# A gated mix of dilated attention and a token MLP on one core: the third w2 load issued ahead of twelve on-chip copies

## The chip, the cores and the metric

The kernel runs on one core of a Trainium2 chip. The metric is device microseconds of one execution. Runs come with the mean clock that TensorE was granted. Before the change: 178.16 us, median of 3 runs (177.43 to 179.45).

## The reference

The reference mixes two branches over x (2048 tokens, 512 features) with a gate per token. Branch A is attention with 32 heads of 16, in which each token looks at 8 earlier tokens at distance 0, 2, ..., 14. Branch B is an MLP along the token axis. Cut to what matters:

```
q, k, v = x @ wqkv                                    # 32 heads of 16
attn = softmax(q . k[s - 2w], w = 0..7)
a = (sum_w attn * v[s - 2w]) @ wo
u = gelu(layernorm(x)^T @ w1 + b1)                    # 512 x 1792, w1: 2048 x 1792
b = (u @ w2 + b2)^T                                   # w2: 1792 x 2048
g = sigmoid(x . gate_w)
out = g * a + (1 - g) * b
```

## The kernel before

The kernel lists its operations with their dependencies and lets a small list scheduler, run when the kernel is built, fix the order on each of the five instruction streams. Of the operations that are ready, the one with the earliest start goes first; among equals, the one with the smaller key, so that a priority of -100 is worth 300 us of critical path:

```python
st = max(clock[e], rtime[op.idx])
k = (st, -bl[op.idx] + 3.0 * op.prio, op.idx)   # bl: longest path to the end
```

All transfers go through one queue, that of SyncE (SP). Two kinds of them matter. The softmax weights are computed in one layout (ATT) and needed in another (ER), chunk by chunk of 512 tokens. So they are copied from SBUF to SBUF, four copies per chunk; the copies of chunks 1 to 3 are twelve, of 288 KB each:

```python
def ld_er(c, r0, nr, rd, nm):
    ds = sch.dsem(nm)
    for g in range(4):
        src = bass.AP(ATT.tensor, ATT.offset + 32 * c * pst5 + r0 * SC, [[pst5, 32], [1, nr * SC]])
        dst = bass.AP(ER.tensor, ER.offset + g * pst5 + (c * (NW + 1) + r0) * SC, [[4 * pst5, 32], [1, nr * SC]])
        sch.dma("sp", mk_dma(dst, src), 32 * nr * SC * 2, ds, reads=rd, writes=["%s_%d" % (nm, g)], deps=er_al, name="d_%s_%d" % (nm, g), prio=-100)
# ... chunk 0 in two halves (er0a, er0b), then its row of reciprocal sums (er0r), then:
for c in range(1, 4):
    ld_er(c, 0, NW + 1, ["att_0", "att_1", "rs_0", "rs_1"], "er%d" % c)
# ... VectorE: per chunk two products of 4.4 us and six smaller steps (the avm to avn steps)
```

The second MLP product takes w2 in eight loads of 896 KB, each for two blocks of 128 tokens, through three buffers. I call the loads w2_0 to w2_7. The third, w2_2, has a buffer of its own that has been free for a long time, so nothing but its place in the queue holds it back:

```python
def ld_w2(j2):
    ds = sch.dsem("w2_%d" % j2)
    al = w2_al[0 if j2 < 2 else 1] if j2 < 3 else ()
    op = sch.dma("sp", mk_dma(W2S[j2 % 3], w2v[:, :, 256 * j2:256 * j2 + 256]), F * 256 * 2, ds,
                 writes=["w2s%d" % (j2 % 3)], deps=al, after=(d_w1[-1:] + d_w2[-1:]) if j2 < 3 else (), name="d_w2_%d" % j2)
    ...
# ... for token block i: two halves (7 matmuls each) with w2, and later 4 matmuls with wo
for half in range(2):
    last_main[0] = A("pe", f_ph3(i, bank, half), 1.515, reads=["ut%d" % ft for ft in ...] + ["w2s%d" % (j2 % 3)], ...)
if i % 2 == 1 and j2 + 3 <= 7:
    ld_w2(j2 + 3)
A("pe", f_wo(i, bank), 0.865, reads=["ot%d" % (i // 4), "wo"], ...)
```

Token block i takes its matmuls with w2 at L840 and those with wo at L849. Blocks 4 and 5 use w2_2. Blocks 12 to 15 need the last chunk of attention from VectorE.

## Time and profile before

| what | value | read from |
|---|---|---|
| span; TensorE busy | 176.4 us; 168.1 us | busy times of the page |
| longest wait of TensorE | 3.79 us, for a DMA of w2 | PE timeline |
| w2_2: issue; landing | 113.16; 121.59 us | SP timeline; landings in the trace |
| er1: landing; needed by VectorE | 105.74; 106.1 us | landings; VectorE's timeline |
| matmuls of 512 columns, 14 in a row | 3.02 us, so 0.216 each | chain of waits |

A landing is the time at which the last DMA engine of a transfer (or group of four copies) counts up its semaphore; the trace holds these times one by one (16 for w2_2, 64 for the four copies of er1).

The first lines to look at are the busy tenths of the page: 40 slices of 4.4 us. PEclk is the granted TensorE clock in tenths.

```profile
PE   7999999999999999999999999974999999999993
DVE  0755369999889996559999999999999999992000
PEclk9999999999999999999999999997899999999999
DMA  5989989930000080809999989989735738001023
```

In the middle of the span TensorE is full except in two slices, the 27th and the 28th, where it falls to 7 and 4. In the 28th and 29th PEclk falls too. The PE timeline of that stretch (start, length, instruction, count, and in brackets the idle time before it and what ended it):

```profile
103.66 2.11 PE L800 MATMUL ps<-arena 128*128 128x512 bf16 x9
105.61 12.25 PE L840 MATMUL ps<-arena 128*128 128x512 bf16 x56
121.64 3.54 PE L840 MATMUL ps<-arena 128*128 128x512 bf16 x8 [3.79 <-DMA arena<-in_B_w_dram]
```

The first 56 matmuls are blocks 0 to 3, four times 14. The next ones wait until w2_2 has landed. Then something else is odd: 8 matmuls fill 3.54 us, which is 0.44 us each and not 0.216. The table of windows (busy time of each engine per stretch, granted clock, DMA share) shows why:

```profile
core 0: us, PE busy (x) PEld busy (x) DVE busy (x) ACT busy (x) POOL busy (x), PEclk, DMA share, GB/s
105.00:117.00 12.00, 12.00 (x57) 5.45 (x56) 11.96 (x4) 0.69 (x1) 0.00 (x0) 1.00 0.97 195
117.00:121.60 4.60, 0.85 (x4) 0.20 (x2) 4.57 (x5) 0.00 (x0) 0.00 (x0) 1.00 0.96 283
121.60:125.00 3.40, 3.36 (x8) 1.19 (x9) 3.33 (x3) 0.00 (x0) 0.00 (x0) 0.50 1.19 290
125.00:130.00 5.00, 5.00 (x25) 2.27 (x24) 5.00 (x2) 0.00 (x0) 0.00 (x0) 1.00 0.29 75
```

Why was w2_2 late? Some lines of the chain of waits and of the SP timeline, in which each SPq line is the issue of a transfer:

```profile
96.71 0.59 SPq L439
...
109.93 1.57 SPq L439
111.51 0.04 issue
111.55 1.57 SPq L439
113.12 0.04 issue
113.16 8.43 DMA arena<-in_B_w_dram
121.59 0.05 issue
121.64 9.36 PE ps L840 x35
```

```profile
91.66 21.46 SPq L439 DMA_DIRECT2D arena<-arena  x16
113.16 7.83 SPq L439 DMA_DIRECT2D arena<-in_B_w_dram  x3
```

The sixteen copies (four of er0r, twelve of er1 to er3) occupy the queue from 91.66 to 113.12. The first issue takes 3.10 us, the next five 0.59 us each, and the later ones mostly about 1.57 us, close to the pace at which the copies land (er1 at 105.74, er2 at 111.29 and er3 at 117.29 us, so 1.4 to 1.5 us a copy). A copy landed 5.8 us after its issue (median of the twelve). Only then does w2_2 go out. VectorE, meanwhile, works through its 32 attention steps without a gap:

```profile
88.14 71.92 DVE L776 TENSOR_TENSOR arena<-arena 128x8192 bf16<-128x8192 bf16 x32
```

### The profile page before, as it was taken

Reading aid. Unit: us, or ns where it says so; the run is one execution under the profiler, and the core shown is the slowest. Engines: PE = TensorE matmul, PEld = TensorE weight load, DVE = VectorE, ACT = ScalarE, POOL = GpSimd, SP = SyncE. Lnnn points to the kernel's source line nnn. Section 1 sums busy time; section 2 is a strip of 40 time slices with the busy share of each in tenths; the row PEclk is TensorE's granted clock in tenths of the full one; section 3 lists DMA queues with packets and bytes.
Section 4 is the critical chain, followed back from the end, with each engine's and each line's share of the span. In section 5 each row is a group of like instructions: output and inputs, shape, how many; then the busy total and the mean of one; then the engine's idle time right before and its main releaser. Section 6 shows DMA issues by size and latency. Waiting matters only on the chain.

```text
span 176.4 us, 2143 instructions
## 1 busy us (share of the span) xinstructions
PE 168.1 (95%) x892; PEld 79.4 (45%) x892; DVE 139.7 (79%) x118; ACT 66.3 (38%) x94; POOL 0.9 (0%) x8
## 2 busy tenths in 40 slices
PE   7999999999999999999999999974999999999993
PEld 2965445455444444444444444421444444444441
DVE  0755369999889996559999999999999999992000
ACT  2376666866285202499231111000002111112174
POOL 1000000000000000000000000000000000000000
PEclk9999999999999999999999999997899999999999
DMA  5989989930000080809999989989735738001023
GB/s 169 324 177 256 156 249 327 291 78 6 0 1 5 8 232 4 238 5 282 231 308 290 197 196 194 190 224 288 183 99 142 204 90 241 30 30 33 30 80 128
DMA packets 43102, 27.42 MB, mean 155 GB/s; under 512 B 7893, under 2 KB 42325, under 8 KB 42709
## 3 DMA queue, kind: packets, MB, share of 16 engines
q1 hardware_dynamic: 43092, 27.28, 62.4%
q8 instruction: 7, 0.11, 0.3%
q14 instruction: 3, 0.02, 0.0%
HBM read 18.88 MB, written 2.10 MB: 119 GB/s over the span
## 4 chain that ended last, share of the span: by engine, by line
PE 58%; SPq 17%; DMA 11%; DVE 8%; ACT 4%; issue 1%
PE ps L840 22%; PE ps L586 14%; SPq L439 12%; PE ps L800 10%; PE ps L849 8%; DMA arena<-in_B_w_dram 5%; SPq L460 4%; PE ps L668 4%; DMA arena<-in_A_x_dram 4%; DMA arena<-in_A_wqkv_dram 3%; DVE arena L713 3%; DVE arena L776 2%; DVE arena L761 2%; ACT arena L727 1%; ACT L727 1%
## 5 line engine op out<-in xcount | busy, mean ns | idle before, releaser
L776 DVE TENSOR_TENSOR arena<-arena 128x2048 bf16<-128x2048 bf16 (+2 forms) x32 | 71.5, 2287 | 0.4
L840 PE MATMUL ps<-arena 128*128 128x512 bf16 x224 | 51.8, 388 | 3.8 <-DMA arena<-in_B_w_dram 3.8
L800 PE MATMUL ps<-arena 128*128 128x512 bf16 x224 | 48.9, 379 | 0.0
L586 PE MATMUL ps<-arena 128*128 128x512 bf16 x176 | 38.9, 379 | 0.6 <-DMA arena<-in_A_x_dram 0.5
L840 PEld LDWEIGHTS ps<-arena 128*128 128x128 bf16 x224 | 22.2, 100 | 31.7 <-DMA arena<-in_B_w_dram 4.3
L661 DVE TENSOR_TENSOR arena<-arena 128x8192 bf16<-128x8192 bf16 x8 | 35.0, 4418 | 1.3 <-ACT arena L597 1.3
L800 PEld LDWEIGHTS ps<-arena 128*128 128x128 bf16 x224 | 21.7, 98 | 26.8 <-issue 0.8
L867 ACT ACTIVATE arena<-ps,arena 128x512 bf16<-128x512 f32 x16 | 12.4, 778 | 55.4 <-PE ps L849 54.9
L586 PEld LDWEIGHTS ps<-arena 128*128 128x128 bf16 x176 | 19.6, 114 | 19.0 <-ACT arena L594 0.9
L597 ACT ACTIVATE arena<-ps 128x512 bf16<-128x512 f32 x32 | 19.0, 597 | 7.1 <-PE ps L586 6.9
L813 ACT ACTIVATE arena<-ps,arena 128x512 bf16<-128x512 f32 x14 | 9.6, 687 | 30.8 <-PE ps L800 30.7
L849 PE MATMUL ps<-arena 128*128 128x512 bf16 x64 | 15.4, 379 | 0.0
L551 DVE BATCH_NORM_STATS2 arena<-arena 128x6 f32<-128x512 bf16 x16 | 9.9, 681 | 6.6 <-DMA arena<-in_A_x_dram 6.6
L849 PEld LDWEIGHTS ps<-arena 128*128 128x128 bf16 x64 | 6.2, 98 | 7.6
L713 DVE TENSOR_TENSOR arena<-arena 128x256 bf16<-128x256 bf16 (+4 forms) x16 | 7.9, 506 | 2.0 <-ACT arena L727 1.7
L594 ACT ACTIVATE arena<-ps 128x512 bf16<-128x512 f32 x12 | 7.2, 596 | 3.5 <-PE ps L586 3.5
L668 PE MATMUL ps<-arena 128*32 128x512 bf16 x128 | 7.5, 380 | 0.0
L698 ACT ACTIVATE arena<-ps 128x1024 bf16<-128x1024 f32 x4 | 4.0, 1021 | 5.0 <-PE ps L638 3.8
L570 DVE TENSOR_SCALAR arena<-arena 128x512 bf16<-128x512 bf16 x16 | 5.3, 406 | 0.0
L668 PEld LDWEIGHTS ps<-arena 128*32 128x32 bf16 x128 | 3.1, 97 | 4.1 <-DVE arena L713 0.4
L513 PE MATMUL ps<-arena 128*128 128x512 bf16 x9 | 4.0, 603 | 1.1 <-POOL arena L426 1.1
L542 DVE COPY arena<-ps 128x512 bf16<-128x512 bf16 x2 | 0.8, 425 | 4.0 <-PE ps L525 3.9
(50 smaller groups left out, 40.2 us busy)
## 6 DMA issues: line engine op xcount, KB each, us to landing
arena<-in_B_w_dram SPq DMA_DIRECT2D x7, 1024.0 KB, 6.8
arena<-in_B_w_dram SPq DMA_DIRECT2D x8, 896.0 KB, 8.9
arena<-arena SPq DMA_DIRECT2D x12, 288.0 KB, 5.8
arena<-in_A_x_dram SPq DMA_DIRECT2D x4, 512.0 KB, 5.1
out_dram<-arena SPq DMA_DIRECT2D x16, 128.0 KB, 1.7
arena<-in_A_wqkv_dram SPq DMA_DIRECT2D x3, 512.0 KB, 4.6
arena<-arena SPq DMA_DIRECT2D x8, 128.0 KB, 3.1
arena<-in_A_wo_dram SPq DMA_DIRECT2D x1, 512.0 KB, 7.7
```

Source lines behind the costliest of these rows:

```text
L439: return lambda e: e.dma_start(dst, src)
L551: A("dve", (lambda t_: (lambda e: e.bn_stats(out=ST6[:, t_, :], in_=X[:, t_, :])))(t), 0.7, reads=["x%d" % t], writes=["st6_%d" % t], name ...
L586: ins = e.matmul(ps[:, bank, :], lhsT=lhsT, rhs=XT[:, sb, dt, :], start=(dt == 0), stop=(dt == 3))
L597: return lambda e: e.activation(out=dst, in_=ps[:, bank, :], func=AF.Copy)
L661: return lambda e: e.tensor_tensor(out=PBL[buf], in0=in0, in1=in1, op=ALU.mult)
L668: ins = e.matmul(ps[32 * c:32 * c + 32, 4 + wl, :], lhsT=RP, rhs=PBL[buf][:, wl, c * 512:(c + 1) * 512], start=(dl == 0), stop=(dl == 3), ...
L713: return A("dve", lambda e: e.tensor_tensor(out=o_, in0=a_, in1=b_, op=op_), dur, reads=rd, writes=wr, name=nm)
L776: A("dve", lambda e: e.tensor_tensor(out=o_, in0=a_, in1=b_, op=op_), dur, reads=rd, writes=wr, name=nm)
L800: ins = e.matmul(ps[:, bank, :], lhsT=W1W[:, slot, st, 128 * e_:128 * e_ + 128], rhs=X[:, st, :], start=(st == 0), stop=(st == NST - 1))
L840: ins = e.matmul(ps[:, bank, :], lhsT=W2S[slot][:, ft, 128 * e_:128 * e_ + 128], rhs=UT[:, ft, :], start=(ft == 0), stop=False)
L849: ins = e.matmul(ps[:, bank, :], lhsT=OT[:, t, 128 * i:128 * i + 128], rhs=WO[:, t, :], start=False, stop=(t == 3))
L867: A("act", (lambda e, i=i, bank=bank: e.activation(out=OUTS[:, i, :], in_=ps[:, bank, :], func=AF.Identity, scale=col(OMG, i), bias=col(C2 ...
```

## The change

The intent: VectorE spends 18.0 us on a chunk (71.92 over 4), so from 88.14 on it needs chunk 2 at about 124 and chunk 3 at about 142 us. TensorE wants w2_2 at about 118, but the copies' priority of -100 puts them first. The change gives the twelve copies priority 0 and lets them wait (in order of issue only) for w2_2. To name w2_2 there, the code that lists the first MLP product and the w2 loads is moved up, unchanged; those moved lines are cut here.

```diff
-        def ld_er(c, r0, nr, rd, nm):
+        def ld_er(c, r0, nr, rd, nm, after=(), prio=-100):
 ...
-                sch.dma("sp", ..., deps=er_al, name="d_%s_%d" % (nm, g), prio=-100)
+                sch.dma("sp", ..., deps=er_al, after=after, name="d_%s_%d" % (nm, g), prio=prio)
 ...
+        (f_ph2, its loop, ld_w2 and the first three ld_w2 calls, moved up from below)
+
         for c in range(1, 4):
-            ld_er(c, 0, NW + 1, ["att_0", "att_1", "rs_0", "rs_1"], "er%d" % c)
+            ld_er(c, 0, NW + 1, ["att_0", "att_1", "rs_0", "rs_1"], "er%d" % c, after=d_w2[2:3], prio=0)
```

## The prediction

> **What bounds the kernel now.** TensorE is busy 168.1 of 176.4 us (table of busy time). Its only long hole is in the second MLP product: the PE timeline shows 56 matmuls of L840 from 105.61 to 117.85 us, then 3.79 us idle until 121.64, released by the DMA of B_w. This is token block 4 waiting for the third w2 load (w2_2). The semaphore landings in the trace show w2_2 landing at 121.59, issued only at 113.16 (SP timeline), behind 16 SBUF-to-SBUF copies issued from 91.66 on; the chain of waits runs through those issues, w2_2, then L840 and L849 to the end.

> The hole costs more than its length. After it, 35 matmuls take 9.36 us, where 14 take 3.02 elsewhere: 7.55 expected, 1.8 lost. The window table shows a granted clock of 0.50 from 121.6 to 125.0 and 1.00 around it. [...] So the whole stall is worth 3.8 + 1.75 = about 5.5 us.

> **What the change does.** No instruction or byte is added or removed. In the scheduler the twelve copies er1 to er3 (288 KB each) now wait for w2_2's issue; the four er0r copies keep their priority and go first. PE, DVE and ACT orders should be unchanged. w2_2 is issued at about 96.7 instead of 113.16 and lands about 3.1 us after w2_1 (98.48; w2_1 itself landed 3.0 after w2_0), so near 101.6. PE needs it at 117.8: that wait goes, and with it the half clock.

> **What it gives back.**
> 1. [...] (every load landed in issue order). So er1 moves back by one load: 105.74 becomes about 108.3. DVE needs it at 106.1 (0.4 us of slack in before), so DVE, which runs L776 without a gap from 88.14 to 160.06, gets a hole of 1.5 to 3 us and ends near 162.4.
> 2. That is probably hidden: the first output product that needs the last chunk (wo_12) started at 170.1 in before and should start near 165.2. About 2.8 us of slack remain.
> 3. The DMA engines are 97% busy from 105 to 117, so the same bytes pass by about the same time: w2_3, landing at 124.77 in before, lands at 123.4 to 124.9. With six token blocks of 3.02 us uninterrupted, PE now wants it at about 123.7. I expect a new wait of 0 to 1.2 us, best guess 0.6[...].

> **Sum.** -3.8 (stall) -1.75 (half clock) +0.6 (w2_3 wait) = -4.9 us: 178.16 to 173.3 us, range 172.2 to 174.9. Faster by over 2%: 0.82; within 2%: 0.17; slower by over 2%: 0.01.

> **What would show each step.** Right: no idle before L840 near 117.8; w2_2 landing near 102; clock 1.00 from 110 to 170; a DVE hole of about 2 us near 106; L840 waiting for B_w by under 1.5 us near 123.7; DVE ending near 162; no wait for DVE before the last L849 matmuls. Wrong: a clock of 0.50 in the middle; DVE ending past 165, with L849 waiting for it; PE order changed.

> **What would make it wrong.** w2_3 landing later than 126, so that the stall only moves by one load (gain then below 3.5 us, "same"). er1 held up by over 5 us, so that DVE becomes the last to finish. [...] A scheduler order that I misjudged, such as w2_2 ahead of er0r (little effect, since er0r is needed only near 104.9).

The sum came to -4.95 us, recorded as -4.9. What is cut are assumptions about when the clock drops and about how the transfers are taken from the queue, which no trace here shows; that the half clock goes with the wait, and that none follows a short one, was my estimate.

## The result, and the profile after

The changed kernel takes 172.31 us (median of 4 runs, 172.0 to 172.55) against 178.38 us (median of 4 runs, 177.43 to 179.45). The ratio is 0.9657, 95% interval 0.9598 to 0.9716. Ratios here are the mean time of one kernel's fast runs over that of the other's of the same rounds, so not quite the ratio of the medians. That is faster, at the low edge of the predicted range. The profile's span fell from 176.4 to 170.8 us.

The busy tenths after:

```profile
PE   7999989999999999999999999999999999999993
DVE  0745369999979999296999998899999999999800
PEclk9999999999999999999999999999999999999999
DMA  5999989960000053443989999998982818001023
```

TensorE and its clock have no hole left in the middle. The PE timeline and the table of windows of the same stretch:

```profile
104.04 1.67 PE L776 MATMUL ps<-arena 128*128 128x512 bf16 x7
105.55 19.80 PE L840 MATMUL ps<-arena 128*128 128x512 bf16 x90
125.19 1.03 PE L849 MATMUL ps<-arena 128*128 128x512 bf16 x3
```

```profile
core 0: us, PE busy (x) PEld busy (x) DVE busy (x) ACT busy (x) POOL busy (x), PEclk, DMA share, GB/s
105.00:117.00 12.00, 11.95 (x57) 5.40 (x56) 10.50 (x4) 0.69 (x1) 0.00 (x0) 1.00 0.98 194
117.00:121.60 4.60, 4.60 (x23) 2.13 (x22) 4.60 (x3) 0.00 (x0) 0.00 (x0) 1.00 0.85 256
121.60:125.00 3.40, 3.40 (x18) 1.51 (x17) 3.33 (x4) 0.00 (x0) 0.00 (x0) 1.00 0.89 234
```

Line L776 is now the first MLP product (it was L800), and VectorE's attention steps are at L816 (they were at L776). The 91 matmuls before the first with wo run through in one stretch; one record is missing from the trace. In the two windows from 117 to 125 TensorE now starts 41 matmuls; before it was 12. The SP timeline shows w2_2 ahead of the twelve copies, and VectorE's timeline shows what that costs:

```profile
91.18 5.21 SPq L439 DMA_DIRECT2D arena<-arena  x4
96.43 0.58 SPq L439 DMA_DIRECT2D arena<-in_B_w_dram  x1
97.06 17.11 SPq L439 DMA_DIRECT2D arena<-arena  x12
114.22 3.99 SPq L439 DMA_DIRECT2D arena<-in_B_w_dram  x2
```

```profile
88.09 17.95 DVE L816 TENSOR_TENSOR arena<-arena 128x8192 bf16<-128x8192 bf16 x8
107.53 53.94 DVE L816 TENSOR_TENSOR arena<-arena 128x8192 bf16<-128x8192 bf16 x24 [1.50 <-DMA arena<-arena]
```

VectorE now waits 1.50 us for er1 and ends at 161.47 instead of 160.06. TensorE needs that only at about 164.25: its last 28 matmuls with wo follow each other from 161.66 on, and the 13th is the first of block 12.

```profile
161.66 6.21 PE L849 MATMUL ps<-arena 128*128 128x512 bf16 x28
```

Landings in the two profiles, in us:

| transfer | before | after | needed in the changed kernel at |
|---|---|---|---|
| w2_1 | 98.48 | 98.16 | |
| w2_2 | 121.59 | 101.97 | 117.6 |
| er1 | 105.74 | 107.44 | 106.0 |
| er3 | 117.29 | 118.70 | |
| w2_3 | 124.77 | 123.19 | 123.7 |

The needs are worked out: 105.55 plus 56 and 84 matmuls of 0.2157 us (3.02 over 14). The chain of waits says who rules the time now:

```profile
PE 83%; DMA 7%; SPq 6%; ACT 2%; issue 1%
```

Before it began with "PE 58%; SPq 17%; DMA 11%; DVE 8%". The part of the chain that led through VectorE and the queue is gone.

### The profile page after: what moved, and what is told of

The parts are those of the page before. It is cut to its first block, busy times and chain, and to the rows that moved or that the text cites. A ratio compares the mean times of both kernels' runs of the same rounds, so it can differ in the third digit from the quotient of the medians.

```text
span 170.8 us, 2127 instructions
## 1 busy us (share of the span) xinstructions
PE 165.0 (97%) x876; PEld 78.6 (46%) x892; DVE 139.7 (82%) x118; ACT 66.2 (39%) x94; POOL 0.9 (1%) x8
## 4 chain that ended last, share of the span: by engine, by line
PE 83%; DMA 7%; SPq 6%; ACT 2%; issue 1%
PE ps L776 28%; PE ps L840 28%; PE ps L586 14%; PE ps L849 8%; SPq L460 5%; PE ps L668 4%; DMA arena<-in_A_x_dram 4%; DMA arena<-in_A_wqkv_dram 3%; SPq L439 1%; ACT L564 1%; PE ps L638 1%; ACT arena L867 0%; ACT arena L594 0%; ACT arena L597 0%; ACT arena L564 0%
## 5 line engine op out<-in xcount | busy, mean ns | idle before, releaser
L816 DVE TENSOR_TENSOR arena<-arena 128x2048 bf16<-128x2048 bf16 (+2 forms) x32 | 71.5, 2287 | 1.8 <-DMA arena<-arena 1.5
L840 PE MATMUL ps<-arena 128*128 128x512 bf16 x220 | 49.8, 379 | 0.2
L776 PE MATMUL ps<-arena 128*128 128x512 bf16 x218 | 48.5, 379 | 0.3
L586 PE MATMUL ps<-arena 128*128 128x512 bf16 x171 | 38.3, 379 | 1.0 <-DMA arena<-in_A_x_dram 0.5
L840 PEld LDWEIGHTS ps<-arena 128*128 128x128 bf16 x224 | 21.9, 98 | 26.4
L776 PEld LDWEIGHTS ps<-arena 128*128 128x128 bf16 x224 | 21.7, 98 | 26.8 <-issue 0.8
L849 PE MATMUL ps<-arena 128*128 128x512 bf16 x63 | 15.4, 379 | 0.1
L849 PEld LDWEIGHTS ps<-arena 128*128 128x128 bf16 x64 | 6.3, 98 | 7.5
L513 PE MATMUL ps<-arena 128*128 128x512 bf16 x9 | 4.0, 603 | 1.1 <-POOL arena L426 1.1
L609 PE MATMUL ps<-arena 128*128 128x256 bf16 x32 | 3.7, 273 | 0.2 <-DMA arena<-in_A_wqkv_dram 0.2
```

What stands on the lines that cost most here:

```text
L586: ins = e.matmul(ps[:, bank, :], lhsT=lhsT, rhs=XT[:, sb, dt, :], start=(dt == 0), stop=(dt == 3))
L776: ins = e.matmul(ps[:, bank, :], lhsT=W1W[:, slot, st, 128 * e_:128 * e_ + 128], rhs=X[:, st, :], start=(st == 0), stop=(st == NST - 1))
L816: A("dve", lambda e: e.tensor_tensor(out=o_, in0=a_, in1=b_, op=op_), dur, reads=rd, writes=wr, name=nm)
L840: ins = e.matmul(ps[:, bank, :], lhsT=W2S[slot][:, ft, 128 * e_:128 * e_ + 128], rhs=UT[:, ft, :], start=(ft == 0), stop=False)
L849: ins = e.matmul(ps[:, bank, :], lhsT=OT[:, t, 128 * i:128 * i + 128], rhs=WO[:, t, :], start=False, stop=(t == 3))
```

## The experiments

Theory A is that of the prediction: the gain is TensorE's removed wait for w2_2 plus the half clock that follows it, and the place of the copies does not matter otherwise. Rival B: the gain comes from holding the copies back, so it grows with the number held back. Rivals C and D concern the clock: it falls after any such wait (C), or for a reason other than TensorE's idleness (D). Rival E: VectorE's new hole costs time. All kernels gave correct results; runs of one group share the runs of the kernel before on their chip. Those were 177.64 us (7 runs) for the first group (split4, split8, split11, fill17), 177.60 us (11 runs, one of them slow) for the second (split10, fill8, extra2, dve2x) and 177.97 us (11 runs) for the last (again, split8b, fill12, fill4). Compare ratios across groups, not times.

### split4, split8, split10, split11: how many copies go first

The base is the changed kernel; AHEAD copies keep their old priority.

```diff
+AHEAD = 4        # or 8, 10, 11
-                ..., after=after, name=..., prio=prio)
+                ..., after=after if 4 * (c - 1) + g >= AHEAD else (), name=...,
+                prio=prio if 4 * (c - 1) + g >= AHEAD else -100)
```

> The change, but with the four copies of chunk 1 (er1) left ahead of w2_2, and only the eight of chunks 2 and 3 behind it. Theory A (the gain is the removed TensorE wait for w2_2 and the half clock that follows it; where the copies stand does not matter as long as w2_2 lands before 117.8 us): w2_2 lands near 108, no TensorE wait, VectorE's hole of 1.5 us near 106 goes, and the time is still that of the change, about 172.3 us. Rival B (the gain comes from holding the copies back, which compete with other work, so it grows with their number): 8 of 12 copies, 8/12 of 6.07 us gained, about 174.3 us.

> Eight copies ahead of w2_2, the four of chunk 3 behind it. Theory A: w2_2 lands near 115, still before 117.8, so again about 172.3 us and no TensorE wait. Rival B: 4/12 of 6.07 us gained, about 176.4 us.

> Ten copies ahead of w2_2, two behind. w2_2 should land near 118.3, so TensorE waits about 0.7 to 1.0 us. Theory A: 172.2 + 0.9 = about 173.1 us, and no run with half clock[...]. Rival C (any wait there drops the clock): 174.8 us. Rival B (2/12 of the gain): about 176.8 us.

> Eleven copies ahead of w2_2, one behind. w2_2 lands one copy (about 1.6 us) earlier than in the kernel before, near 120.0, so TensorE waits about 2.2 us. Theory A[...]: no half clock, 172.3 + 2.2 = about 174.5 us. Rival C (the clock falls after any such wait): half clock for 3.4 us again, 1.75 us more, about 176.2 us. Rival B: 1/12 of the gain, about 177.9 us.

| copies ahead | w2_2 landed | TensorE's wait for it | median us | ratio to before, 95% interval |
|---|---|---|---|---|
| 4 (split4) | 109.44 | none | 172.35 (4 runs) | 0.9712 (0.9669 to 0.9756) |
| 8 (split8) | 115.36 | none | 172.02 (4 runs) | 0.9693 (0.9649 to 0.9736) |
| 10 (split10) | 117.43 | 0.48 us | 172.71 (6 runs) | 0.9721 (0.9680 to 0.9763) |
| 11 (split11) | 119.73 | 2.52 us | 174.96 (4 runs) | 0.9886 (0.9818 to 0.9954) |

The PE timeline of split11 shows the rest of the old wait:

```profile
105.01 12.25 PE L843 MATMUL ps<-arena 128*128 128x512 bf16 x55
119.77 7.73 PE L843 MATMUL ps<-arena 128*128 128x512 bf16 x35 [2.52 <-DMA arena<-in_B_w_dram]
```

Rival B falls: with only four copies held back (split8) the whole gain is there, where it expected 176.4 us. What counts is whether w2_2 lands before TensorE asks for it; past that point each further copy in front moves the landing back (117.43, 119.73 and 121.59 us with 10, 11 and 12 ahead), and the wait grows with it. Split4 has a small wait of 0.22 us for w2_3, the wait that I had predicted for the change itself. In split11 the clock was at 0.999 or 1.0 in three runs (174.70 to 175.13 us) and at 0.99 in one (176.40 us). So neither C (always) nor my expectation (no half clock after so short a wait) holds strictly. The runs of the kernel before in this group split in the same way: five at 0.989 or 0.990 with 177.13 to 178.02 us, two at 0.999 with 176.36 and 176.25 us.

### fill17, fill12, fill8, fill4: keep TensorE busy while it waits

The base is the kernel before; nothing is moved. Useless matmuls of ones into an unused PSUM bank fill the first part of the hole.

```diff
+            if i == 3:
+                last_main[0] = A("pe", f_warm_on(17, 3), 0.01, reads=["ones"], writes=["bank3"],
+                                 after=[last_main[0]], name="fill", prio=0)      # or 12, 8, 4
             if i % 2 == 1 and j2 + 3 <= 7:
                 ld_w2(j2 + 3)
```

> The kernel before, nothing moved, but 17 matmuls of ones into an unused PSUM bank are put into TensorE's hole ahead of the first matmul that needs w2_2 (17 x 0.216 = 3.67 us; they wait for nothing). The wait for w2_2 still ends at about 121.6. Theory A: the clock stays at 1.00, so 1.75 us of the time come back although w2_2 is as late as ever: about 176.6 us against 178.4. Rival D (the clock falls for another reason at that time, load or transfers, and not because TensorE is idle): no change, about 178.4 us, with a clock of 0.50 near 122.

Measured: 176.27 us (4 runs, clock 0.997 or more in all), ratio 0.9935 (0.989 to 0.998). The windows of fill17:

```profile
117.00:121.60 4.60, 4.47 (x21) 1.88 (x20) 4.57 (x4) 0.00 (x0) 0.00 (x0) 1.00 1.03 293
121.60:125.00 3.40, 3.40 (x18) 1.56 (x16) 3.33 (x3) 0.00 (x0) 0.00 (x0) 1.00 1.20 290
```

The DMA share and the rate from 121.6 to 125.0 are the same as before (1.20 and 290 GB/s against 1.19 and 290), w2_2 is nearly as late as before (121.18 against 121.59), but the clock is 1.00 (0.50 before). So D falls: with the same transfers, and TensorE busy instead of idle for 3.79 us, the clock stayed up in all 4 runs, where it fell in 5 of 7 of the kernel before. Doing useless work makes the kernel 1.4 us faster (a small difference, but the interval excludes none).

> As fill17, but with 8 matmuls of ones (1.73 us): the wait for w2_2 ends as late as in the kernel before, and TensorE is idle for about 2.1 us of it. The runs so far show two levels of one kernel: the kernel before at a granted clock of 0.99 (177.1 to 178.0 us, 5 of 7 runs, idle 3.8 us) and at 0.999 (176.3 us, 2 of 7); split11 at 0.99 in 1 of 4 (idle 2.5 us). Theory A2[...]: with 2.1 us idle no run drops, all near 176.3 us. Theory A as predicted[...]: likewise no run. Rival D (the idle time does not matter): mixed as the kernel before, median about 177.6 us.

(A2 is theory A with an estimate of mine for the idle time that brings the drop. How I came to it, here and for fill12 and fill4, is cut, since no trace here shows what it assumed.)

Measured: 177.22 us over 6 runs (ratio of the fast ones 0.9919, 0.9855 to 0.9982), in two groups: 176.22, 175.59 and 175.68 us at a clock of 1.0, and 178.23, 178.51 and 178.57 us at 0.99. (The last two are labelled slow, since they are over 1.5% above the fastest; I use them only for the count.) The idle time in the profile was 1.88 us. Both A and A2 had no drop here, so this is a miss.

> The kernel before with 12 matmuls of ones in the hole, so that TensorE is idle for about 1.2 us of the wait. fill8 (1.9 to 2.1 us idle) showed the half clock in 3 of 6 runs[...]. [...] all six at 0.998 or more, about 176.2 us. If any hole of over 1 us can drop it, some runs at 0.99 and near 178.

Measured: 176.22 us (ratio 0.9889, 0.9852 to 0.9927), all 5 runs at 1.0. The idle time was 1.66 us in its profile, more than the 1.2 us expected. w2_2 landed when it does in the kernel before (121.62 against 121.59), but TensorE came to the hole about 0.44 us earlier (its first L840 matmul starts at 105.17 against 105.61).

> The same with 4 matmuls: idle about 2.9 us. By the new estimate[...] about 4 or 5 of 6 runs are at 0.99, near 177.8 us, the rest at 0.998 or more, near 176.2 us. If the share does not grow with the idle time (split11, 2.5 us, had 1 of 4; fill8, 2.0 us, 3 of 6), it would be half or less.

Measured: 177.77 us (ratio 0.9968, 0.9923 to 1.0013, so the times alone show no difference); four of 6 runs at 0.99 (177.76 to 178.43 us), two at 0.998 or 1.0 (176.03 and 176.65 us). The profiled run, with 3.10 us idle, is one of the four:

```profile
117.00:121.60 4.60, 1.50 (x8) 0.50 (x6) 4.57 (x4) 0.00 (x0) 0.00 (x0) 1.00 1.02 290
121.60:125.00 3.40, 3.40 (x9) 1.17 (x8) 3.33 (x3) 0.00 (x0) 0.00 (x0) 0.51 1.20 290
```

### extra2: a longer wait

The base is the kernel before, with two more copies (256 KB each, into a w1 buffer that is no longer used) ahead of w2_2.

```diff
+        for g in range(2):
+            src = bass.AP(ATT.tensor, ATT.offset + 96 * pst5, [[pst5, 32], [1, NW * SC]])
+            dst = bass.AP(W1W.tensor, W1W.offset + 32 * g * pst5 + NST * 256, [[pst5, 32], [1, NW * SC]])
+            sch.dma("sp", mk_dma(dst, src), ..., deps=sch.users(["w1s1"]), name="d_xtra%d" % g, prio=-80)
         for j2 in range(3):
             ld_w2(j2)
```

> The kernel before with two more copies (256 KB each, 1.4 us each by the rate of the others) into a dead weight buffer, ahead of w2_2. TensorE's wait grows by about 2.8 to 6.6 us. Theory A and A2: [...] every run shows the half clock (granted clock at or below 0.99, no run at 0.999), and the time is about 177.8 + 2.8 = 180.6 us. If the drop is a matter of chance unrelated to the idle length, two of seven runs would again be at 0.999 and 1.75 us shorter.

Measured: 180.56 us (6 runs), ratio 1.0168 (1.0122 to 1.0214), every run at a clock of 0.98 or below. TensorE waited 6.51 us. The windows of extra2:

```profile
117.00:121.60 4.60, 0.00 (x0) 0.00 (x0) 4.57 (x4) 0.00 (x0) 0.00 (x0) 0.82 0.91 247
121.60:125.00 3.40, 1.51 (x4) 0.58 (x5) 3.33 (x3) 0.00 (x0) 0.00 (x0) 0.50 1.16 306
125.00:130.00 5.00, 5.00 (x20) 2.06 (x19) 5.00 (x2) 0.00 (x0) 0.00 (x0) 0.82 0.60 149
```

The clock falls while TensorE is still idle (0.82 on average from 117.0 to 121.6, with no matmul), is 0.50 all the way to 125.0, and rises only after that (0.82 on average to 130.0). The time is as expected, and all runs show the drop.

Taken together, the runs with a granted clock of 0.990 or below:

| TensorE's idle time in the profile | kernels | runs with half clock |
|---|---|---|
| 0.5 us or less near 117 | the change, split4, split8, split10, fill17, dve2x, again, split8b | 0 of 36 |
| 1.66 us | fill12 | 0 of 5 |
| 1.88 us | fill8 | 3 of 6 |
| 2.52 us | split11 | 1 of 4 |
| 3.10 us | fill4 | 4 of 6 |
| 3.79 us | the kernel before | 27 of 29 (one of the 27 is labelled slow) |
| 6.51 us | extra2 | 6 of 6 |

The idle time is that of the one profiled run of each kernel; the profiled runs of fill8 and split11 were at 1.0 and 0.999, so those of their runs with half clock can have been idle for longer or shorter. In the counts no run of a kernel with up to 1.66 us had the half clock, and all with 6.51 us had it; in between, from 1.88 to 3.79 us, some runs of one kernel had it and some not. What decides between them was not shown.

In the kernel before the trace also records when the clock changed: it fell at 121.58 us, after 3.73 us without a matmul (117.85 to 121.58), and rose at 124.99, so it was at half for 3.41 us. In the profiled run of fill4 it was 0.51 from 121.6 to 125.0 after a hole of only 3.10 us. What was expected of fill12 (no drop) and fill4 (four or five of 6) came.

### dve2x: how much slack VectorE has

The base is the changed kernel; the first product of chunk 1 is computed twice.

```diff
+                if (c, wh) == (1, 0):
+                    tt(P, ..., ALU.mult, 0.01, v_res + er_res(c, wh), r_, "avm_twice")
                 ev = sub(P, 0, [(4 * SC, 4), (2 * SC, 2), (1, SC)])
```

> The change, with the first product of chunk 1 on VectorE computed twice (4.4 us more, result unchanged). In the changed kernel VectorE ends at 161.47 and the first product that needs its last chunk would start at about 164.4, so about 3.0 us of slack are left. Theory A: 4.4 - 3.0 = 1.4 us slower than the change, about 173.7 us, with a TensorE wait for VectorE of about 1.4 us ahead of the last L849 matmuls. Rival E (VectorE has no slack, its 1.5 us hole already costs): 4.4 us slower, about 176.7 us. If its slack were much larger, no change, 172.3 us.

Measured: 173.05 us (6 runs), ratio 0.9730 (0.9692 to 0.9769), where the change itself has 0.966 in its two own comparisons. The PE timeline of dve2x:

```profile
161.08 2.75 PE L852 MATMUL ps<-arena 128*128 128x512 bf16 x12
164.67 3.63 PE L852 MATMUL ps<-arena 128*128 128x512 bf16 x16 [0.83 <-DVE arena L816]
```

The sixteen matmuls of blocks 12 to 15 now wait 0.83 us for VectorE. Of 4.4 us added, 0.83 came through, so the slack was about 3.6 us in that run (3.4 us if the wait is read from the start of one matmul to that of the next). The expected 1.4 us was too much, in the main because VectorE's wait for er1 was 0.76 us there and not 1.50. Rival E falls.

### again, split8b: the change beside a variant without VectorE's hole

The kernels are the change itself and split8 once more, with no further edit.

> The changed kernel itself, for a direct comparison on one chip with a variant. Theory A: every run at a granted clock of 0.998 or more, about 172.3 us; and no wait for the fourth w2 load above 0.3 us.

> split8 again (eight copies ahead of w2_2, four behind), beside the change on the same chip. Theory A: within 0.3 us of the change, although VectorE ends about 1.5 us earlier, since TensorE works without a hole in both. If VectorE's hole cost anything in the change, split8b would be about 1.5 us faster, 170.8 us.

Measured on the same chip: the change 171.90 us (4 runs, 171.84 to 172.16), ratio 0.966 (0.9624 to 0.9696); split8b 172.38 us (4 runs, 172.15 to 172.66), ratio 0.9685 (0.9648 to 0.9722). VectorE has no hole in split8b, and yet it is not faster; it is 0.5 us slower, outside the 0.3 us that I allowed. Its profile shows no new wait, and on another chip split8 ran in 172.02 us. The two profiles show where their difference arises: the spans are 170.86 and 170.13 us, 0.73 apart, and VectorE's first attention step already starts at 88.16 us against 87.42, 0.74 apart and before any transfer that the two kernels order differently. Over all 14 profiles that start lies between 87.27 and 88.16 us, so up to 0.9 us of scatter comes from the part of the kernel that no edit touches. No experiment points to a version that beats the change: TensorE has no hole left in the middle to close.

## Why the prediction was right

**The wait for w2_2: right.** It was put at 3.8 us, the idle time in one profile. What it costs is better read from the starts of the matmuls: the 57th L840 matmul was due at 105.61 + 56 x 0.2157 = 117.69 and started at 121.64, so 3.95 us. In the same way the hole is 3.77 us in fill8, 3.95 in fill17, 4.13 in fill4 and 4.41 in fill12. So the wait changes by some tenths from run to run. On the last chip the kernel before with the clock kept up (fill12, 176.22 us) and the change (171.90 us) differ by 4.32 us.

**The half clock: the right size, but it also came after shorter waits.** In the profile the 35 matmuls after the hole took 9.20 us from start to start (121.64 to 130.84), where 35 x 0.2157 = 7.55 was due: 1.65 us lost. On the last chip it was worth 177.97 - 176.22 = 1.75 us, just the predicted term. In the first group it was 177.64 - 176.27 = 1.37 us; two of the seven runs of the kernel before had no half clock there, and the median of the other five, 177.85 us, is 1.58 above fill17. That no half clock follows a shorter wait was my estimate, and it failed: the half clock came in 3 of 6 runs of fill8 (1.88 us idle in the profile), 1 of 4 of split11 (2.52 us) and 4 of 6 of fill4 (3.10 us). Why one kernel has two levels is not shown.

**The new wait for w2_3: did not come in the change.** This is the term that was mis-sized: "+0.6 (w2_3 wait)", with a landing from 123.4 to 124.9. It landed at 123.19, 0.5 us before the need at 123.7. The step that failed is "the same bytes pass by about the same time": they passed sooner than in the kernel before, by 1.6 us. From the landing of er0r to that of w2_3, with the same bytes between, it is 25.5 to 25.9 us in the five profiles with all twelve copies ahead of w2_2 (the kernel before, 25.50, and the fills) and 23.7 to 24.7 us in the eight of the change (24.21) and its variants. So with the new order these transfers took 1 to 2 us less; why was not tested. That the wait was close is shown by split4, with its 0.22 us.

**The order of the landings: right.** In the profiles of both kernels every load, and every group of four copies, landed in issue order (after: w2_1 at 98.16, er0r at 98.98, w2_2 at 101.97, er1 at 107.44 us). w2_2 landed at 101.97 (predicted 101.6), er1 at 107.44 (108.3), and VectorE's hole was 1.50 us (1.5 to 3).

**VectorE's slack: right.** Predicted 2.8 us; 2.8 us in the profile of the change (164.25 - 161.47), and about 3.5 us by dve2x, where VectorE's hole was 0.74 us shorter. The orders on TensorE, VectorE and ScalarE did stay as they were.

The sum can be taken from the two profiles alone: 3.95 + 1.65 = 5.60 us, and 0.06 us because TensorE reached the stage that much earlier, where the spans differ by 5.65. So the stall explains the gain, without a remainder. The prediction had 5.5 for the stall, almost the same, and took off 0.6 for w2_3 that was not lost; hence -4.9. The medians of the result differ by 6.07 us, in a scatter of 2 us among the runs of the kernel before. (The last chip gives -4.32 - 1.75 = -6.07 too, but there the two terms are the two parts of one difference, cut at fill12, so their sum is no check.)

What stays open: what decides whether the clock drops when TensorE is idle for 1.88 to 3.79 us; why the transfers passed sooner in the new order; and why fill8's two groups lie so far apart (178.23 us in the fast run with half clock, 175.83 us on average in those without, so 2.4), when the half clock, if it lasts 3.41 us as in the profile of the kernel before, costs only 1.7.

## What to carry to other kernels

In one transfer queue, order by when each transfer is needed, and not by a priority given to a whole group: the last four of the twelve copies were needed some 24 us later than the load behind them (142 against 118), and moving only those four behind it gave the whole gain. Price a TensorE wait of a few microseconds with the slow clock that can follow it (here 1.65 us on top of 3.95), read from the clock column and not from busy time. When a load moves ahead, check who waits for what it displaces: here VectorE lost 1.5 us and had 2.8 us to spare.
